# Loading ScalarE's function table ahead of two small input transfers in a single-core decode layer

## The chip, the cores and the metric

The kernel runs on one core of a Trainium2 chip. The metric is the time of one execution on the device in microseconds (us); smaller is better.

## The reference

One decoding step for four sequences: adaptive layer norm, attention over a window of cached keys and values, adaptive layer norm again, and a feed-forward block with ReLU. Everything is bfloat16. Cut to what matters:

```python
W = min(4096, max(256, Sk // 4))           # 1024 cached positions, 8 key/value heads, 32 query heads
mod = (silu(c) @ w_mod).reshape(4, 6, 1, -1)
sa, ca, ga, sb, cb, gb = (mod[:, i] for i in range(6))
h = layernorm(x) * (1 + ca) + sa
x = x + ga * attention(h, k_cache, v_cache, wq, wo)    # softmax over the last W positions
h = layernorm(x) * (1 + cb) + sb
x = x + gb * (relu(h @ w1) @ w2)
```

`c` and `x` (called `A_x`) are 4 x 512 numbers, 4 KB each. The weights and the two caches are 32 MB.

## The kernel before

SyncE issues all large loads in one queue, in the order of their use: two key blocks, the modulation weights `wmod_sb`, the query weights, six more key blocks, eight value blocks, the output weights, the feed-forward weights. ScalarE issues the two small transfers first and then loads its function table.

```python
cx_sb = work.tile([2 * B, D], bf16, name="cx_sb")
nc.scalar.dma_start(out=cx_sb[0:B, :], in_=c)
nc.scalar.dma_start(out=cx_sb[B:2 * B, :], in_=A_x.rearrange("b o d -> (b o) d"))
# ...
for gi in range(KAHEAD):                   # KAHEAD = 2
    load_k(gi)                             # 1 MiB each, on nc.sync
nc.sync.dma_start(out=wmod_sb[:], in_=w_mod.rearrange("(p t) n -> p t n", t=DT))   # 3 MiB
# ... wq, keys 2 to 7, values 0 to 7, wo, w1, w2: all on nc.sync
nc.scalar.preload_act_table_set("natural_log_exp_and_others")
# ... constants on GpSimd and VectorE
tp0 = psA.tile([P, DT, 2 * B], bf16, tag="t", name="tp0")
for t in range(DT):                        # L177: the first work of TensorE
    nc.tensor.transpose(out=tp0[:, t, :], in_=cx_sb[:, t::DT], identity=ident_bf[0:2 * B, 0:2 * B])
nc.scalar.activation(out=a_c[:], in_=cT, func=ACT.Abs)              # cT: the c half of tp0
nc.scalar.activation(out=t_c[:], in_=a_c[:], func=ACT.Exp, scale=-1.0)
# ... VectorE makes silu(c) of it: siluT32
kts_pending = [k_transposes(gi) for gi in range(KAHEAD)]            # L202: 64 transposes
# ... L236: the first matmuls that need siluT32 and wmod_sb
```

TensorE takes its instructions in program order: the transposes of `cx_sb`, the 64 transposes of the first two key blocks, then the modulation matmuls.

## Time and profile before

| Item | Before |
|---|---|
| Median time, in the rounds with the changed kernel | 85.91 us (85.81 to 85.98, 6 runs) |
| Span of the profiled run | 84.1 us |
| Moved by DMA | 32.13 MB |
| Last feed-forward weights landed | 79.42 us |
| `ACT_TABLE_LOAD` | 1.60 to 2.88 us |
| `cx_sb` first used by TensorE | 4.49 us |
| First key transposes | 5.99 us |
| Modulation matmuls (L236) start | 15.94 us, after 4.40 us of idle time |

The span runs from the first to the last instruction of the trace; the measured time is 1.8 us more. How to read the table: the first five microseconds belong to the change, the 4.40 us are the room behind it, and 79.42 us is the moment after which only a few microseconds of work remain. The prediction shows the lines themselves.

### The profile page before, as it was taken

What the parts mean: (1) busy time and instruction counts of PE and PEld (TensorE: products, weight loads), DVE (VectorE), ACT (ScalarE), POOL (GpSimd) and SP (SyncE); (2) the same over time, 40 slices, a digit from 0 to 9 for tenths busy, and PEclk for the clock granted to TensorE, in tenths of its full rate; (3) what the DMA queues carried; (4) which work ended last, traced back from release to release, by engine and by line L of the source; (5) the groups of instructions that cost most, each with busy time, mean ns of one, the idle gap of its engine ahead of it and who ended that gap; (6) DMA issues with size and microseconds to landing.
All of it is one profiled execution on the core that took longest, in us unless ns stands there. A gap on an engine that the chain in (4) does not pass through costs nothing.

```text
span 84.1 us, 2367 instructions
## 1 busy us (share of the span) xinstructions
PE 57.5 (68%) x1064; PEld 47.4 (56%) x1064; DVE 26.4 (31%) x73; ACT 23.5 (28%) x37; POOL 5.2 (6%) x20
## 2 busy tenths in 40 slices
PE   0029940499729899999999329996454478598840
PEld 0029940248629739977778029996452058588720
DVE  0144480030330103645665768500003020241420
ACT  2314670003020004977798196300000010001000
POOL 6980000000000000000000000000000000000000
PEclk9999999957955555999999995696555555555555
DMA  0999998999999999999999999999999999999500
GB/s 2 333 401 452 503 421 386 444 421 444 421 394 405 433 433 413 413 413 425 425 413 409 425 425 421 405 433 421 425 409 409 425 432 425 413 398 406 210 0 2
DMA packets 4077, 32.13 MB, mean 382 GB/s; under 512 B 476, under 2 KB 612, under 8 KB 996
## 3 DMA queue, kind: packets, MB, share of 16 engines
q1 hardware_dynamic: 4052, 31.99, 91.7%
q8 instruction: 8, 0.13, 0.6%
q10 hardware_dynamic: 16, 0.01, 0.0%
q14 instruction: 1, 0.01, 0.0%
HBM read 31.99 MB, written 0.00 MB: 381 GB/s over the span
## 4 chain that ended last, share of the span: by engine, by line
DMA 64%; PE 25%; DVE 3%; issue 2%; SPq 1%; ACT 1%; DVEq 0%
DMA w<-in_B_w_dram 24%; DMA v<-in_A_v_cache_dram 24%; DMA wmod_sb<-in_w_mod_dram 16%; PE ktp L202 9%; PE qT_ps L302 4%; PE sc_ps L214 4%; PE mT L253 2%; PE mT L255 2%; PE z_ps L470 2%; PE m_ps L236 2%; SPq L81 1%; PE m_ps L239 1%; PE gb_ps L244 1%; PE st_ps_var L269 1%; ACT lnv L286 0%
## 5 line engine op out<-in xcount | busy, mean ns | idle before, releaser
L202 PEld LDWEIGHTS <-k 128*128 128x128 bf16 x256 | 17.3, 110 | 3.9 <-issue 2.5
L202 PE MATMUL ktp<-ident_k,k 128*128 128x128 bf16 x256 | 18.4, 241 | 1.2 <-DMA k<-in_A_k_cache_dram 1.2
L207 ACT COPY kT<-ktp 128x1024 bf16<-128x1024 bf16 x16 | 15.5, 1016 | 13.2 <-PE ktp L202 12.1
L205 DVE COPY kT<-ktp 128x1024 bf16<-128x1024 bf16 x16 | 11.1, 691 | 11.6 <-PE ktp L202 11.3
L340 PE MATMUL oT_ps<-pT,v 128*128 128x16 bf16 x256 | 7.3, 172 | 2.5 <-issue 1.9
L340 PEld LDWEIGHTS <-v 128*128 128x128 bf16 x256 | 7.1, 100 | 2.7 <-issue 2.0
L214 PE MATMUL sc_ps<-kT,qpad 128*32 128x512 bf16 x64 | 5.6, 445 | 0.4 <-DVE qpad L306 0.4
L357 PE MATMUL pT_ps<-ident_bf,p_rep 128*128 128x128 bf16 x32 | 3.1, 278 | 2.9 <-DVE p_rep L351 2.9
L357 PEld LDWEIGHTS <-p_rep 128*128 128x128 bf16 x32 | 2.7, 127 | 3.4 <-DVE p_rep L351 3.4
L302 PE MATMUL qT_ps<-hT,wq_sb 128*128 128x4 bf16 x128 | 3.6, 166 | 1.4 <-DVE ab L295 1.4
L302 PEld LDWEIGHTS <-wq_sb 128*128 128x128 bf16 x128 | 3.5, 104 | 1.5 <-issue 1.5
L236 PE MATMUL m_ps<-wmod_sb,siluT 128*32 128x512 bf16 x16 | 1.3, 435 | 4.4 <-DMA wmod_sb<-in_w_mod_dram 4.4
L409 ACT COPY y<-y_ps 128x256 f32<-128x256 f32 x1 | 0.4, 372 | 11.4 <-DVE y L408 11.4
L404 PE MATMUL y_ps<-wo_sb,o 128*32 128x512 bf16 x16 | 2.1, 619 | 2.0 <-DMA wo_sb<-in_A_wo_dram 1.1
L177 PE MATMUL tp<-ident_bf,cx_sb 8*128 8x8 bf16 x4 | 0.3, 168 | 4.5 <-DMA cx_sb<-in_A_x_dram 4.5
L236 PEld LDWEIGHTS <-siluT 128*32 128x32 bf16 x16 | 0.4, 95 | 4.7 <-issue 4.5
L382 DVE TENSOR_TENSOR oT_sb<-oT_ps,rb 128x128 bf16<-128x128 f32 x1 | 0.3, 292 | 8.6 <-PE oT_ps L340 8.6
L416 PEld LDWEIGHTS <-wo_sb 128*128 128x128 bf16 x64 | 2.5, 121 | 0.6 <-DMA wo_sb<-in_A_wo_dram 0.6
L416 PE MATMUL y_ps<-o,wo_sb 128*128 128x4 bf16 x64 | 2.4, 173 | 0.5 <-DMA wo_sb<-in_A_wo_dram 0.5
L177 PEld LDWEIGHTS <-cx_sb 8*128 8x128 bf16 x4 | 0.2, 110 | 4.5 <-issue 4.5
L351 DVE TENSOR_TENSOR p_rep<-e_sb,mi 128x512 int32<-128x512 int32 x4 | 2.5, 685 | 0.7 <-ACT e_sb L346 0.7
L459 PE MATMUL u_ps<-ab,w 128*128 128x8 bf16 x56 | 2.4, 181 | 0.4 <-DMA w<-in_B_w_dram 0.4
(107 smaller groups left out, 57.0 us busy)
## 6 DMA issues: line engine op xcount, KB each, us to landing
k<-in_A_k_cache_dram SPq DMA_DIRECT2D x8, 1024.0 KB, 25.8
v<-in_A_v_cache_dram SPq DMA_DIRECT2D x8, 1024.0 KB, 19.9
wq_sb<-in_A_wq_dram SPq DMA_DIRECT2D x2, 2048.0 KB, 18.0
wo_sb<-in_A_wo_dram SPq DMA_DIRECT2D x4, 1024.0 KB, 19.9
wmod_sb<-in_w_mod_dram SPq DMA_DIRECT2D x1, 3072.0 KB, 13.7
w<-in_B_w_dram SPq DMA_DIRECT2D x1, 1792.0 KB, 21.7
w<-in_B_w_dram SPq DMA_DIRECT2D x1, 768.0 KB
w<-in_B_w_dram SPq DMA_DIRECT2D x1, 640.0 KB, 20.1
```

What stands on the lines that cost most here:

```text
L202: nc.tensor.transpose(out=tp[:, ii, :], in_=k_tiles[gi][:, iq * IQ + ii, :], identity=ident_k)
L205: nc.vector.tensor_copy(out=dst, in_=tp[:])
L207: nc.scalar.copy(out=dst, in_=tp[:])
L214: nc.tensor.matmul(out=sc_ps[hw * CG:(hw + 1) * CG, half * HALF:(half + 1) * HALF], lhsT=qpad[:, b, par, hw, :], rhs=kT[:, half * (NI // 2 ...
L236: nc.tensor.matmul(out=m4_ps[k * CG:(k + 1) * CG, :], lhsT=siluT32[:, t, :], rhs=wmod_sb[:, t, k * D:(k + 1) * D], start=(t == 0), stop=(t ...
L302: nc.tensor.matmul(out=qT_v[:, hq, :], lhsT=wq_sb[:, t, hq * Dh:(hq + 1) * Dh], rhs=hT[:, t, :], start=(t == 0 and hq == 0), stop=(t == DT ...
L340: nc.tensor.matmul(out=oT_ps[:, hw, par].rearrange("p b r -> p (b r)"), lhsT=v_tiles[h][:, i, :], rhs=pT[:, i, c0:c0 + B * rep], start=(fi ...
L351: nc.vector.tensor_tensor(out=p_w[:, ws, :], in0=e_w[:, ws].unsqueeze(2).to_broadcast([P, WQ // 2, B]), in1=mi4[:].unsqueeze(1).to_broadca ...
L357: nc.tensor.transpose(out=tp[:, ii, :], in_=p_rep[:, i // 2, :, i % 2], identity=ident_bf[:])
L404: nc.tensor.matmul(out=y4_ps[q0:q0 + CG, :], lhsT=o4[:, l, g % 2, g // 2, :], rhs=wo_sb[:, g, l, :], start=(g == 0 and l < 4), stop=(g == ...
L416: nc.tensor.matmul(out=y_ps[:, m, :], lhsT=wo_sb[:, g, l, m::DT], rhs=o4[:, l, g % 2, g // 2, 0:B], start=False, stop=(g == NP - 1 and l = ...
L459: nc.tensor.matmul(out=u_ps[:, m - m0].rearrange("p s b -> p (s b)"), lhsT=w1_cols(t, m), rhs=ab[:, t].rearrange("p s b -> p (s b)"), star ...
```

## The change

The intent is to have the table ready as early as possible: the load is the first instruction of ScalarE, and the two small transfers are issued behind it. The risk is that they have to wait for it.

```diff
+    nc.scalar.preload_act_table_set("natural_log_exp_and_others")
 
     cx_sb = work.tile([2 * B, D], bf16, name="cx_sb")
     nc.scalar.dma_start(out=cx_sb[0:B, :], in_=c)
@@
-    nc.scalar.preload_act_table_set("natural_log_exp_and_others")
     ident_bf = const.tile([P, P], bf16, name="ident_bf")
```

## The prediction

> **What bounds the kernel now.** I began with the page, to see whether any engine is near full, then read the chain of waits that ended last, and only then the first eight microseconds, where the change is.
>
> ```profile
> PE 57.5 (68%) x1064; PEld 47.4 (56%) x1064; DVE 26.4 (31%) x73; ACT 23.5 (28%) x37; POOL 5.2 (6%) x20
> DMA  0999998999999999999999999999999999999500
> DMA 64%; PE 25%; DVE 3%; issue 2%; SPq 1%; ACT 1%; DVEq 0%
> ```
>
> The first line is each engine's busy time and its share of the 84.1 us span. ScalarE (ACT) is busy for 28% and no compute engine is near full. The second is the DMA engines' busy share, in tenths, in 40 slices of 2.1 us: empty in the first slice, eight or nine tenths until the 37th, then over. The page gives 32.13 MB moved, 31.99 MB of it read from HBM. From about 2.0 us to the last landing at 79.42 us that is 32.1 / 77.4 = 415 GB/s, with no gap. The third is the chain's shares: 64% is transfers. So this kernel is one long input stream with a head (before the first byte) and a tail (after the last byte).
>
> The chain in order of time (start in us, length in us, what) shows both:
>
> ```profile
> 0.73 0.66 SPq L81
> ...
> 1.46 0.58 SPq L81
> ...
> 2.07 13.73 DMA wmod_sb<-in_w_mod_dram
> ...
> 39.39 19.88 DMA v<-in_A_v_cache_dram
> ...
> 59.28 20.14 DMA w<-in_B_w_dram
> ...
> 79.46 1.31 PE z_ps L470 x30
> ```
>
> The head is the SyncE queue (SPq) issuing the first two key transfers. ScalarE's two small transfers, `c` and `A_x`, are not on this chain at all, nor is the table load. The tail is 30 matmuls, 0.30 and 0.29 us of VectorE and the output transfer. The measured 85.94 us is 1.84 us more than the span, a part that the change does not enter.
>
> Now the start (timeline: start, length, engine, line, what; in brackets idle time before it and what ended it):
>
> ```profile
> 0.73 0.55 ACTq L71 DMA_DIRECT2D cx_sb<-in_c_dram  x1
> 0.73 1.30 SPq L81 DMA_DIRECT2D k<-in_A_k_cache_dram  x2
> 1.31 0.26 ACTq L72 DMA_DIRECT2D cx_sb<-in_A_x_dram  x1
> 1.60 1.28 ACT L129 ACT_TABLE_LOAD   x1 [1.60 <-PEq L498]
> 4.49 0.26 PE L177 MATMUL tp<-ident_bf,cx_sb 8*128 8x8 bf16 x4 [4.49 <-DMA cx_sb<-in_A_x_dram]
> 4.78 0.18 ACT L180 ACTIVATE a_c<-tp 128x16 f32<-128x16 bf16 x1 [1.90 <-PE tp L177]
> 5.99 5.37 PEld L202 LDWEIGHTS <-k 128*128 128x128 bf16 x64 [1.33 <-DMA k<-in_A_k_cache_dram]
> 6.58 0.23 DVE L189 TENSOR_TENSOR siluT<-tp,f_c 128x16 bf16<-128x16 bf16 x1
> 15.94 1.27 PE L236 MATMUL m_ps<-wmod_sb,siluT 128*32 128x512 bf16 x16 [4.40 <-DMA wmod_sb<-in_w_mod_dram]
> ```
>
> The load runs from 1.60 to 2.88 us, and ScalarE then idles 1.90 us until the transposes of `cx_sb` have finished on TensorE. So its early end is worth nothing today: it is already hidden behind the landing of `A_x`. The next two gaps are the cushions of this branch. TensorE waits until 5.99 us for the first key block whatever happens to `cx_sb`. It then sits idle 4.40 us before the modulation matmuls (L236), which wait for the 3 MB `wmod_sb`. `siluT`, the product of the small transfers, is ready at 6.58 + 0.23 = 6.81 us and first used at 15.94 us, 9.1 us later.
>
> **What the Trainium skill says.** "ScalarE: Activation LUTs", section "What ACT_TABLE_LOAD costs", gives about 1283 ns for the load and about 1380 ns for a drain, 2.66 us a switch. The trace agrees on the load (1.28 us); the drain is not visible, since ScalarE's next work waits for TensorE until 4.78 us. "Perfetto Trace Analysis", section "Sequencer Loop", says that the sequencer pushes engine instructions into a queue and starts control instructions itself. A transfer issued behind a table load then would not have to wait for the load to end. The trace before cannot confirm this: ScalarE issues nothing after its load. The same page, in its HWDGE section, says that the descriptor generator is shared by the two issuing queues and locked for one at a time. The trace agrees in kind: `c` took 0.55 us to issue beside the first key transfer, `A_x` 0.26 us. "DMA: Bandwidth & Descriptors", section "Queues, rings and completion order", says that each DMA engine alternates between the queues packet by packet, so two 4 KB transfers should not sit behind megabytes of another queue. Here they were used at 4.49 us, before the first key block landed, with the key queue already full; one instance, in agreement.
>
> **The change part by part.** Nothing is removed or added; three ScalarE instructions change order.
>
> *Table load to the front.* It starts where `c` started, 0.73 us, and ends near 0.73 + 1.28 = 2.01 instead of 2.88 us. Gain on the path: nothing, for `a_c` waits for TensorE.
>
> *Small transfers behind it.* From the end of the `A_x` issue (1.31 + 0.26 = 1.57 us) to its use (4.49 us) is 2.92 us; I keep that delay. Three cases:
> (a) the issue only waits for the load to be handed over: a few hundredths later, use near 4.5 us;
> (b) the issue waits for the load's end at 2.01: two issues at 0.26 to 0.4 us each, done near 2.6 to 2.8, use near 5.5 to 5.7, transposes done by about 6.0, just as the first key block lands;
> (c) it waits for the skill's drain too: all of (b) 1.38 us later, use near 7.1, and the key transposes start near 7.4 instead of 5.99, 1.4 us late.
> I take (a), at about even odds, because of the sequencer section; but the answer hardly depends on it. The worst, 1.4 us, comes out of 4.40 us of idle time before L236 and leaves 3.0. `siluT` would be ready near 9.5 against 15.94 us. In none of the cases does it get to the chain.
>
> *Issue on the SyncE side.* The first key issue took 0.66 us, with `c` being issued beside it. The third to eighth key transfers took mostly 0.53 or 0.54 us where they stood alone in the timeline. If the sharing cost the first 0.66 - 0.54 = 0.12 us, and `c` now comes behind, the whole stream may start about 0.1 us earlier. This is the only term on the path, and I count 0.08 of it.
>
> Sum: 85.94 - 0.08 = 85.86; I predict 85.85 us.
>
> **Rivals.** *A later wait in the transfer queue.* In the program of before the transfers take eight completion semaphores in turn, in the order `c`, k0, `A_x`, k1, `wmod_sb`, two of `wq_sb`, k2; then k3 must wait for `c`, k4 for k0, k5 for `A_x`, k6 for k1 and k7 for `wmod_sb`. The SyncE queue's own waits show the ones that bite:
>
> ```profile
> SPq L81 <- DMA wmod_sb<-in_w_mod_dram: 6.8, 1, 6.8
> SPq L81 <- DMA k<-in_A_k_cache_dram: 2.4, 2, 1.3
> ```
>
> (waiter, what it waits for, us in total, times, longest.) With `c` and `A_x` later, k3 and k5 may be issued later, and if the two small transfers move in the order, k5 may even wait for `wmod_sb`, until 15.8 us. That would hurt only if the queue ran dry. Before k3 there are k0, k1, `wmod_sb`, `wq_sb` and k2 in it: 1 + 1 + 3 + 4 + 1 = 10 MiB, 10.5 MB, or 25 us at 415 GB/s. Even with k5 held to 15.8 us, 4 MiB of `wq_sb` and 3 MiB of keys are still in front, 17 us. So 0 us; were I wrong, and the stream stopped for a microsecond, 86.9 us.
>
> *The branch of the small transfers becomes the bound.* That takes more than 4.4 us of push on TensorE's key transposes, that is, `cx_sb` usable later than about 10 us. Nothing in the trace makes it so late; it would cost what it overshoots, say 86.5 us.
>
> *ScalarE becomes a bound early,* because its evacuations of the key transposes (first at 7.07 us) slide. They share the same 4.40 us. About 85.9 us.
>
> *A shorter head.* If the head is cut by the whole extra 0.12 us and the 0.04 of the second issue (0.58 against 0.54), 85.78 us. No larger gain is in reach: the stream still has its 77 us.
>
> **Range and chances.** The three runs of before lie within 0.17 us. Adding a tenth or two for the head and for a stream that differs a little from build to build gives 85.55 to 86.15. Faster by over 2% needs 84.2 us, which means 1.7 us out of a head whose only movable term is 0.16: 1%. Slower by over 2% needs 87.7 us, more than the worst rival that I can build: 2%. The rest, 97%, is within 2%.
>
> **What would show it.** Right: the load at 0.73 us and 1.28 us long; the chain still from key issue to `wmod_sb`, values and the last weights, landing near 79.3 to 79.5 us; L236 still released by `wmod_sb` near 15.8 us; the first key issue near 0.55 us. The start of the `c` issue tells (a), (b) and (c) apart: near 0.8, near 2.0, near 3.4 us. Wrong: a zero in the DMA row between slices 2 and 37, L236 released by `siluT`, or the first key block landing well away from 5.97 us.

## The result and the profile after

The changed kernel took 86.00 us in the median (85.82 to 86.07, 6 runs), against 85.91 us before. The ratio is 1.0007, with a 95% interval of 0.9993 to 1.002: the same. Ratios here are the mean time of one kernel's runs over that of the other's of the same rounds, so not quite the ratio of the medians that are quoted.

These are the busy times, the DMA row and the shares of the chain from the page after:

```profile
PE 57.6 (68%) x1064; PEld 47.4 (56%) x1064; DVE 26.3 (31%) x73; ACT 23.5 (28%) x37; POOL 5.2 (6%) x20
DMA  0999998999989999999999999999999999999500
DMA 64%; PE 26%; DVE 3%; issue 2%; SPq 1%; ACT 1%; DVEq 0%
```

No busy time has moved by more than 0.1 us, no share by more than one per cent, and the DMA row has no new gap. The timeline of the start of the changed kernel shows what did move (start, length, engine, line, what):

```profile
0.73 1.28 ACT L69 ACT_TABLE_LOAD   x1 [0.73 <-PEq L498]
0.76 0.55 ACTq L72 DMA_DIRECT2D cx_sb<-in_c_dram  x1
1.34 0.26 ACTq L73 DMA_DIRECT2D cx_sb<-in_A_x_dram  x1
4.55 0.26 PE L177 MATMUL tp<-ident_bf,cx_sb 8*128 8x8 bf16 x4 [4.55 <-DMA cx_sb<-in_A_x_dram]
4.84 0.18 ACT L180 ACTIVATE a_c<-tp 128x16 f32<-128x16 bf16 x1 [2.83 <-PE tp L177]
15.84 1.49 PE L236 MATMUL m_ps<-wmod_sb,siluT 128*32 128x512 bf16 x16 [4.46 <-DMA wmod_sb<-in_w_mod_dram]
```

The load starts at 0.73 instead of 1.60 us. The issue of `c` starts at 0.76 us, 0.03 us after the load has started and 1.25 us before it ends: the queue of ScalarE (ACTq) did not wait for the load. So `cx_sb` is used at 4.55 instead of 4.49 us, and ScalarE, with its table ready 0.87 us earlier, idles 2.83 us before its first activation where it idled 1.90. The gain became idle time, because what ended the wait was TensorE's transposes, as before. L236 is still released by `wmod_sb`.

The end of the chain of waits in the changed kernel (start, length, what):

```profile
39.55 19.82 DMA v<-in_A_v_cache_dram
...
59.38 20.17 DMA w<-in_B_w_dram
...
79.60 1.31 PE z_ps L470 x32
```

The last weights land at 79.56 us (before: 79.42), and the span is 84.2 us (84.1). That 0.1 us is inside the scatter of the spans of the six runs, 84.0 to 84.2.

### The profile page after: what moved, and what is told of

Read it like the earlier page. It is cut to its first block, busy times and chain, and to the rows that moved or that the text cites. A ratio compares the mean times of both kernels' runs of the same rounds, so it can differ in the third digit from the quotient of the medians.

```text
span 84.2 us, 2367 instructions
## 1 busy us (share of the span) xinstructions
PE 57.6 (68%) x1064; PEld 47.4 (56%) x1064; DVE 26.3 (31%) x73; ACT 23.5 (28%) x37; POOL 5.2 (6%) x20
## 4 chain that ended last, share of the span: by engine, by line
DMA 64%; PE 26%; DVE 3%; issue 2%; SPq 1%; ACT 1%; DVEq 0%
DMA w<-in_B_w_dram 24%; DMA v<-in_A_v_cache_dram 24%; DMA wmod_sb<-in_w_mod_dram 16%; PE ktp L202 9%; PE qT_ps L302 4%; PE sc_ps L214 4%; PE m_ps L236 2%; PE mT L253 2%; PE z_ps L470 2%; PE mT L255 1%; SPq L82 1%; PE m_ps L239 1%; PE gb_ps L244 1%; PE st_ps_var L269 1%; ACT lnv L286 0%
## 5 line engine op out<-in xcount | busy, mean ns | idle before, releaser
L207 ACT COPY kT<-ktp 128x1024 bf16<-128x1024 bf16 x16 | 15.5, 1015 | 12.8 <-PE ktp L202 11.8
L357 PE MATMUL pT_ps<-ident_bf,p_rep 128*128 128x128 bf16 x32 | 3.3, 290 | 2.9 <-DVE p_rep L351 2.9
L357 PEld LDWEIGHTS <-p_rep 128*128 128x128 bf16 x32 | 2.9, 135 | 3.4 <-DVE p_rep L351 3.4
L302 PE MATMUL qT_ps<-hT,wq_sb 128*128 128x4 bf16 x128 | 3.7, 166 | 1.4 <-DVE ab L295 1.4
L236 PE MATMUL m_ps<-wmod_sb,siluT 128*32 128x512 bf16 x16 | 1.5, 503 | 4.5 <-DMA wmod_sb<-in_w_mod_dram 4.5
L302 PEld LDWEIGHTS <-wq_sb 128*128 128x128 bf16 x128 | 3.6, 104 | 1.5 <-issue 1.5
L236 PEld LDWEIGHTS <-siluT 128*32 128x32 bf16 x16 | 0.4, 101 | 4.8 <-issue 4.6
```

Of the source, the lines that this page charges most:

```text
L207: nc.scalar.copy(out=dst, in_=tp[:])
L236: nc.tensor.matmul(out=m4_ps[k * CG:(k + 1) * CG, :], lhsT=siluT32[:, t, :], rhs=wmod_sb[:, t, k * D:(k + 1) * D], start=(t == 0), stop=(t ...
L302: nc.tensor.matmul(out=qT_v[:, hq, :], lhsT=wq_sb[:, t, hq * Dh:(hq + 1) * Dh], rhs=hT[:, t, :], start=(t == 0 and hq == 0), stop=(t == DT ...
L357: nc.tensor.transpose(out=tp[:, ii, :], in_=p_rep[:, i // 2, :, i % 2], identity=ident_bf[:])
```

## The experiments

"The same" fits two stories. One: the change has no effect on the small transfers, so nothing follows. Two: the small transfers could come several microseconds later and still nothing would follow. The experiments ask how much the branch may slip, what a slip really costs, and what a table load costs when it is not hidden. The line numbers of held0 to held20 are five higher than those of the changed kernel (L241 there is L236), those of held4_rows seven higher; those of no_preload are one lower than in the kernel before.

**held0: the small transfers wait for the end of the load.** From the changed kernel:

```diff
     cx_sb = work.tile([2 * B, D], bf16, name="cx_sb")
+    hold = const.tile([P, 1024], f32, name="hold")
+    nc.vector.memset(hold[:], 0.0)
+    nc.scalar.copy(out=cx_sb[0:1, 0:16], in_=hold[0:1, 0:16])
     nc.scalar.dma_start(out=cx_sb[0:B, :], in_=c)
```

Expected:

> The two small transfers are held until ScalarE's table load has really ended: one small ScalarE copy behind the load writes a corner of cx_sb, and the c transfer must wait for it (numbers in cx_sb are overwritten by c, so the result stays right). c should be issued near 2.3 us instead of 0.76, and cx_sb used near 5.9 instead of 4.55 us. Main theory (the branch has more than 4 us of cushion): key transposes start near 6.2 instead of 5.98, L236 still waits for wmod_sb near 15.8, time 85.9 to 86.0. Rival (table and transfers are on the path): up to 1.4 us longer, 87.3. Second question, the issue times: if the c issue slows the first key issue by sharing the descriptor generator, the first key issue is now 0.54 us and c about 0.26; if a queue's first issue is simply longer, they stay at 0.66 and 0.55.

Measured: 85.91 us (85.85 to 85.92, 4 runs) against 85.88 us, ratio 1.0001 (0.9986 to 1.0016). From the timeline of held0:

```profile
2.25 0.54 ACTq L77 DMA_DIRECT2D cx_sb<-in_c_dram  x1
7.74 0.26 PE L182 MATMUL tp<-ident_bf,cx_sb 8*128 8x8 bf16 x4 [7.74 <-DMA cx_sb<-in_A_x_dram]
```

This is the slow case (b) of the prediction, and the time is the same. L241 starts at 15.85 us, released by `wmod_sb`, with 2.35 us of idle time left in front of it. But `cx_sb` was used at 7.74 us, not near 5.9, and the key transposes began at 7.93, not near 6.2: from the end of the `A_x` issue (3.09 us) it took 4.65 us, not 2.92. The second question is answered against sharing: the first key issue, now without any issue of ScalarE beside it, still took 0.65 us, and `c` took 0.54 us.

**held4: held back further.** As held0, with four ScalarE copies of 128 x 1024 numbers in front of the small copy:

```diff
     nc.vector.memset(hold[:], 0.0)
+    for _ in range(4):
+        nc.scalar.copy(out=hold[:], in_=hold[:])
     nc.scalar.copy(out=cx_sb[0:1, 0:16], in_=hold[0:1, 0:16])
```

Expected:

> As held0 with four ScalarE copies of 1024 elements (about 1.04 us each) in front of the small one: c issued near 6.5 us, cx_sb used near 9.5, key transposes start near 9.8 instead of 5.98 us, 3.8 us late. The idle time before L236 was 4.46 us, so the cushion theory says that about 0.6 us of it are left, L236 still released by wmod_sb, time 85.9 to 86.1. The rival, no cushion, says about 89.8.

Measured: 86.24 us (86.21 to 86.33, 4 runs) against 85.88 us, ratio 1.0043 (1.0028 to 1.0058). From the timeline of held4:

```profile
7.16 0.26 ACTq L78 DMA_DIRECT2D cx_sb<-in_A_x_dram  x1
14.73 0.26 PE L182 MATMUL tp<-ident_bf,cx_sb 8*128 8x8 bf16 x4 [14.73 <-DMA cx_sb<-in_A_x_dram]
20.51 1.05 PE L241 MATMUL m_ps<-wmod_sb,siluT 128*32 128x512 bf16 x16
```

The issue came where it was expected, but `cx_sb` was usable only 7.31 us after its end. So this run went further than planned: the key transposes were 8.94 us late (14.92 against 5.98), and L241 started at 20.51 instead of 15.84 us, 4.67 us late, no longer waiting for any transfer (there is no bracket behind it). The expectation that it would still wait for `wmod_sb` was missed. Even so the spans are 84.1 to 84.2 us, those of the kernel before, and the last weights land at 79.41 us. A delay of 4.67 us behind the room of 4.46 us was taken up in full before the end. The 0.36 us by which the time grew lie outside the span: it is 2.1 us more than the span in each of the four runs, where it is 1.8 us in the kernel before. What these 0.3 us are stays open.

**held10 and held20: held back until it must hurt.** The same edit with `range(10)` and `range(20)`. Expected of held10:

> Ten copies: c issued near 12.7 us, cx_sb used near 15.7, key transposes 9.9 us late, so L236 about 5.4 us late. Theory A, the rival as the prediction put it (the overshoot over the 4.4 us is paid in full): about 91.4 us. Theory B (later waits of TensorE for transfers, 0.8 + 1.2 + 0.5 + 0.4 + 0.3 us before values, output and FFN weights, and perhaps 1.8 more, take up part, because the stream of transfers goes on): 86.5 to 88.3 us, with the last weights landing still near 79.5 us.

Expected of held20:

> Twenty copies: c issued near 23 us, cx_sb used near 26, key transposes 20 us late, L236 about 15.8 us late. Theory A: about 101.8 us. Theory B: the same minus 3 to 5 us, 97 to 99 us; TensorE should wait for no transfer after L236. The transfer queue holds k0, k1, wmod_sb, wq_sb, k2 and k3 before the first transfer that waits for a small one, 11.5 MB or 28 us, so the DMA row should show no gap before about 45 us even now; later gaps may come from buffers that the keys free late.

Measured: held10 90.23 us (89.59 to 90.74, 4 runs), ratio 1.0501 (1.0449 to 1.0553); held20 99.59 us (98.87 to 100.22, 4 runs), ratio 1.162 (1.158 to 1.166). Both branches were later than expected (9.83 and 18.54 us instead of 5.4 and 15.8), because the small transfers again landed late. So the times expected beforehand do not decide: held10 lies outside theory B's 86.5 to 88.3 us and nearer to theory A's 91.4. The modulation matmuls of held10 and the DMA row of the page of held20:

```profile
25.67 1.05 PE L241 MATMUL m_ps<-wmod_sb,siluT 128*32 128x512 bf16 x16
```

```profile
DMA  4799989999999999999999999999999991000000
```

| | L236/L241 late against the changed kernel | paid (median against before) | taken up |
|---|---|---|---|
| held0 | 0.0 us | 0.0 us | all |
| held4 | 4.67 us | 0.36 us, none of it in the span | 4.3 us or more |
| held10 | 9.83 us | 4.35 us | 5.5 us |
| held20 | 18.54 us | 13.71 us | 4.8 us |

Set against the lateness that was really reached, theory A, that all lateness behind the first room is paid, is refuted: it would give 90.6 us for held4, 95.7 for held10 and 104.4 for held20. Theory B holds in kind: about five microseconds more are taken up downstream. The table sets the lateness of the profiled run against the median of four; in the profiled runs alone the span grew by 4.4 us (held10, 88.6) and 12.8 us (held20, 97.0), so that 5.4 and 5.7 us were taken up.

Where they come from can be read in two stretches. From the first transposes of the softmax result (L357, or L362) to the end of the span it takes 34.4 us in the changed kernel, 30.4 in held10 and 30.6 in held20, 3.8 to 4.0 us less. In the changed kernel TensorE's matmuls wait in this stretch for values, output weights and feed-forward weights for 0.76 + 1.16 + 0.48 + 0.40 + 0.30 = 3.1 us; in held10 and held20 not once. The other 0.7 to 0.9 us are not accounted for. The rest is a faster middle: from the start of L236 to those transposes it takes 33.96 us in the changed kernel, 32.50 in held10 and 32.03 in held20, so 1.5 to 1.9 us less. Most of that lies right behind L236: up to the first query matmul (L302) it takes 9.47 us in the changed kernel, at a granted clock (the share of its full speed that TensorE was given) of 0.70 in this stretch, 8.04 in held10 at 0.87 and 8.15 in held20 at 0.80. The same stretch took 7.91 us in held0 at 0.89, and 11.53 in load_behind_abs (below) at 0.50. So the time goes with the granted clock; that the clock is the cause is argued, since no run sets it alone.

The DMA row of held20 is cut in slices of 97.0 / 40 = 2.4 us. It is full until slice 33, which is about 80 us, and the stream ends near 81 us, one to two microseconds later than before. Even with `cx_sb` held to 29 us it had no gap that shows, only a lower rate between 50.9 and 60.6 us (375 GB/s against 420 in the changed kernel, about one microsecond of stream): the SyncE queue waited for `c` (1.9 us in all) and for the transposes that free key buffers (21.2 us), but there were always megabytes issued in front of it. The end, 16 us later, is set by the engines alone.

**load_behind_abs: a table load in the open.** From the kernel before:

```diff
-    nc.scalar.preload_act_table_set("natural_log_exp_and_others")
@@
     nc.scalar.activation(out=a_c[:], in_=cT, func=ACT.Abs)
+    nc.scalar.preload_act_table_set("natural_log_exp_and_others")
```

Expected:

> From the kernel before: the table load now comes behind the first activation (Abs), with its own wait for nothing else, so that it lies in the open between Abs and Exp; the build puts one more load, of another set, in front of Abs, where it is hidden. This measures the exposed cost: Exp starts after Abs (about 5.0 us) plus 1.3 us if a switch costs the load alone, plus 2.7 us if a drain of 1.38 us belongs to it. siluT ready near 8.1 or 9.5 instead of 6.81 us, used at 15.9. Main theory (cushion): time 85.9 to 86.1, no matter which. Rival (a late table load reaches the end): 87.2 to 88.6.

Measured: 85.92 us (85.77 to 85.95, 4 runs) against 85.93 us, ratio 0.9994 (0.9977 to 1.0012). From ScalarE's timeline:

```profile
4.76 0.18 ACT L179 ACTIVATE a_c<-tp 128x16 f32<-128x16 bf16 x1 [1.89 <-PE tp L176]
4.97 1.28 ACT L180 ACT_TABLE_LOAD   x1
6.26 0.21 ACT L182 ACTIVATE t_c<-a_c 128x16 f32<-128x16 f32 x1
```

A switch between two activations costs 1.28 us and some hundredths: `Exp` starts 0.01 us after the load's end. The drain of 1.38 us of the prediction's case (c) does not show. `siluT` was ready at 7.42 + 0.23 = 7.65 us, and the time is the same: a load in the middle of this branch is as free as one at its head. The slower stretch behind L236 that was named above, 2.1 us longer than in the changed kernel, was free as well.

**no_preload: loads where the program cannot hide them.** From the kernel before:

```diff
-    nc.scalar.preload_act_table_set("natural_log_exp_and_others")
```

The build then adds five loads by itself. Expected:

> From the kernel before: no explicit load; the build then puts five, of two sets, in front of Abs, of each of the two Ln and of the Exp behind each Ln. The first is hidden as before. The two at the first layernorm lie in the chain from L236 to the scores (near 24 us), the two at the second behind s_ps (near 75 us), before ffn1. If the theory holds that only what lies behind the last weights' landing, or pushes TensorE past all later waits for transfers, is paid, then the first pair (about 1.3 or 2.6 us exposed) is taken up by later waits and costs 0 to 1 us, and the second pair delays ffn1 (u_ps, near 76 us) by about 2.6 us; ffn1 ends near 79.1 us today and z_ps waits 0.3 us for the last weights, so that some 2 us are paid: 87.5 to 89. If loads are hidden wherever they stand: 86.0.

Measured: 86.97 us (86.21 to 87.14, 4 runs) against 85.93 us, ratio 1.0098 (1.0043 to 1.0152). From ScalarE's timeline of the second layer norm:

```profile
71.14 1.28 ACT L445 ACT_TABLE_LOAD   x1
77.31 0.30 ACT L445 ACTIVATE mm<-mm,eps_t 128x4 f32<-128x4 f32 x1 [4.89 <-DVE mm L444]
77.63 1.28 ACT L446 ACT_TABLE_LOAD   x1
78.92 0.20 ACT L446 ACTIVATE rstd<-mm 128x4 f32<-128x4 f32 x1
```

The load before `Ln` ran at 71.14 us, six microseconds before its activation had its data. The load before `Exp` had the `Ln` in front of it and was paid. I had counted both as exposed, so the expectation of 87.5 to 89 us was too high. At the first layer norm both loads were exposed (26.15 and 27.76 us): there the built program has a wait for VectorE's result in front of the load, and at the second layer norm the wait is on `Ln` itself, behind the load. `z_ps` started at 79.86 us and ran without a wait for weights, to 81.6 us instead of 80.8 in the kernel before. The exposed loads are not its only lateness in this profiled run: from the first modulation matmul to those of the variance it took 9.53 us at a granted clock of 0.50, where the kernel before took 7.44 at 0.77. The same 2.1 us cost nothing in load_behind_abs; here the loads and the slow stretch together may have used up the slack, and the runs do not separate them. Three runs at a granted clock of 0.703 to 0.707 took 86.96 to 87.14 us, with spans of 84.9 to 85.1; the one at 0.733 took 86.21, with the span of the kernel before, 84.1. Such a dependence on the clock would fit a kernel whose end is set by TensorE; four runs are few. And 0.1 to 0.3 us of the loss lie outside the span, which is 2.0 to 2.1 us shorter than the time.

**held4_rows: what delays a small transfer.** From held4:

```diff
-    nc.sync.dma_start(out=wmod_sb[:], in_=w_mod.rearrange("(p t) n -> p t n", t=DT))
+    wmod_src = w_mod.rearrange("(p t) n -> p t n", t=DT)
+    for t in range(DT):
+        nc.sync.dma_start(out=wmod_sb[:, t, :], in_=wmod_src[:, t, :])
```

Expected:

> held4 with one more edit: wmod_sb comes in four transfers with rows of 6 KB instead of one with rows of 24 KB. In the runs with held transfers, from the end of the A_x issue to the use of cx_sb took 4.65 us beside key rows of 8 KB (held0), 7.31 us beside the 24 KB rows of wmod_sb (held4), 5.42 us at the change from wmod_sb to the 16 KB rows of wq_sb (held10) and 4.37 us near the end of wq_sb (held20). Theory R (a small transfer waits for rows of the other queue that are under way, so the wait grows with their size): 4 to 5 us here, cx_sb used near 11.5 to 12.5 us. Rival (it waits for bytes already queued, whatever the rows): again about 7.3 us, near 14.7. Time in either case that of held4 or less: 85.9 to 86.3.

Measured: 86.68 us (86.63 to 86.81, 4 runs) against 85.96 us, ratio 1.0084 (1.0069 to 1.0099). From the timeline of held4_rows:

```profile
11.83 0.26 PE L184 MATMUL tp<-ident_bf,cx_sb 8*128 8x8 bf16 x4 [11.83 <-DMA cx_sb<-in_A_x_dram]
```

The issue of `A_x` ended at 7.41 us, so it took 4.42 us, where the same issue at the same time took 7.31 us beside rows of 24 KB. Theory R's prediction of 4 to 5 us holds; the rival's 7.3 us does not. The edit also changes the number of transfers and with it the semaphores, so these two runs alone leave the size of the rows the likely, not the only possible, cause.

The packets settle more of it. The kept traces hold every DMA packet with its start, length and size. The two small transfers are 8 packets of 1 KB and 8 of 4 bytes, and they run among packets of the SyncE queue, each of which is one row:

| | SyncE's packets meanwhile | one takes (median) | first packet of `c` to the end of the last of `A_x` |
|---|---|---|---|
| held4_rows | 6 KB | 0.23 us | 0.94 us |
| held0 | 8 KB | 0.31 us | 1.09 us |
| held20 | 8 KB | 0.31 us | 1.24 us |
| held10 | 16 KB | 0.61 us | 2.04 us |
| held4 | 24 KB | 0.91 us | 3.74 us |

The four groups of small packets (the data of `c`, the 4 bytes behind them, the same for `A_x`) begin about one large packet apart: at 10.40, 11.36, 12.27 and 13.22 us in held4, and at 10.30, 10.58, 10.81 and 11.08 us in held4_rows. So in this part theory R is shown, in four runs with the same number of transfers and one with more. It also explains the 4.37 us of held20: its packets stood beside key rows of 8 KB, not beside `wq_sb` as the expectation took it. The other part does not go with the rows: the first packet of `c` starts 2.8 to 3.3 us after the end of its issue in all five runs, and 0.4 us after it in the changed kernel, where the stream has not yet begun. Its cause stays open. (The packets' clock may lie half a microsecond off that of the instructions; the comparison of runs does not depend on it.)

The kernel itself is slower than held4, not faster as I expected: its span is 84.5 us, the last weights land at 79.72 us, 0.3 us later than in held4, and it too has some 2.2 us outside the span. Why is open.

**swap_cx: which issue is the long one.** From the changed kernel, the two lines of the small transfers exchanged:

```diff
-    nc.scalar.dma_start(out=cx_sb[0:B, :], in_=c)
     nc.scalar.dma_start(out=cx_sb[B:2 * B, :], in_=A_x.rearrange("b o d -> (b o) d"))
+    nc.scalar.dma_start(out=cx_sb[0:B, :], in_=c)
```

Expected:

> The changed kernel with the two small transfers in the other order, A_x first. If the first issue of a queue is the longer one whatever it carries, A_x now takes about 0.55 us and c 0.26; if the c transfer itself is the costly one, c keeps 0.55. The first key issue stays at 0.66 us. cx_sb used near 4.5 us, time 85.8 to 86.1.

Measured: 85.97 us (85.92 to 86.16, 4 runs) against 85.96 us, ratio 0.9997 (0.9981 to 1.0014). From ScalarE's timeline:

```profile
0.76 0.55 ACTq L72 DMA_DIRECT2D cx_sb<-in_A_x_dram  x1
1.34 0.26 ACTq L73 DMA_DIRECT2D cx_sb<-in_c_dram  x1
```

`A_x` is now the long one. The first issue of ScalarE's queue takes 0.55 us whatever it carries. The first key issue stayed at 0.66 us, as expected; `cx_sb` was used at 4.73 us, 0.2 us later than expected, without effect.

No version came out of this that beats the two kernels.

## Why the prediction was right, point by point

**The bound.** Right. The stream of loads ends at 79.4 to 79.6 us in both kernels, and near 81 us even in held20. That only a shorter stream, head or tail would have shortened the time follows from the chain of waits; no run here shortens one of them.

**The load at the front.** Right: 0.73 us, 1.28 us long, and the earlier end turned into idle time (2.83 us, of which 1.90 were there).

**Case (a) for the small transfers.** Right: the issue of `c` came at 0.76 us, beside the load. The prediction took this case at even odds, so this was half luck; the time did not depend on it, as held0 shows for the other case. The start times fit a sequencer that passes the load on and goes to the next instruction, but show nothing of its inside.

**The cushion.** Right, and too small: the prediction allowed a lateness of 4.4 us at the key transposes. held4 was 8.94 us late there without a longer span.

**The delay of 2.92 us that (b) and (c) kept.** This step failed: "I keep that delay." held0 is case (b), and it measured 4.65 us; further on it was 7.31 us. The argument that two small transfers do not sit behind megabytes came from one instance at the very start, when the stream had only just begun. The small packets did get their turns among the large ones, but each turn cost one row of the other queue, up to 0.91 us, and the first turn came about 3 us after the issue. Had (b) come true, `cx_sb` would have been used at 7.7 rather than 5.5 to 5.7 us. It would still have cost nothing, as held0 shows, so the forecast did not depend on it.

**The 0.12 us of sharing, of which 0.08 were counted.** This step failed: "If the sharing cost the first 0.66 - 0.54 = 0.12 us". The first key issue takes 0.64 to 0.66 us in every kernel, whether ScalarE's first issue starts beside it or only at 2, 7, 13 or 24 us; the sign that the prediction named, "the first key issue near 0.55 us", did not come. Nor was the 0.55 us of `c` a sign of a shared generator, as the prediction read it: in held4 `c` took 0.55 us with no SyncE issue beside it. The swap shows that on ScalarE's queue the first issue is the long one (0.55 against 0.26 us); that the first key issue is long for the same reason is the likely reading. Without this term the sum is 85.94 us. The measured ratio, 1.0007, says that the true term is near zero.

**The rival of a later wait in the transfer queue.** Rightly put at 0 us. In the changed program the order of the semaphores is k0, `c`, `A_x`, k1, so that k4 and k5 wait for the small transfers. In held4 the SyncE queue did wait 3.8 us for `c` and 1.4 us for `A_x`, and the last weights came no later.

**The rival of the branch as the bound.** Its price was mis-sized: "it would cost what it overshoots". About the first five microseconds of overshoot cost nothing in the span, mostly because TensorE later stands waiting for transfers; beyond that nearly each microsecond is paid (from held10 to held20 8.71 us more lateness, 8.4 us more span).

## What to carry to other kernels

A setup instruction is worth moving only if something waits for it: look at what ended the idle time behind it, here a matmul that waited for data, and the gain can be read off as zero. In a kernel that streams its weights, the slack of an early branch is not only the idle time in front of its first consumer: the later waits for transfers add to it (here 3.1 us of the 5.4 to 5.7 taken up), so look at those too before you price a delay. Issue small inputs first: at the start they were usable 2.9 us after their issue, in the running stream 4.4 to 7.3 us.

## What the Trainium skill lacked or had wrong

- "ScalarE: Activation LUTs", "What ACT_TABLE_LOAD costs": a load of about 1283 ns is right (1.28 us in every run). The further drain of about 1380 ns was not there: in load_behind_abs `Abs` ended at 4.94 us, the load ran from 4.97 to 6.25, and `Exp` began at 6.26; in no_preload `Ln` ended at 27.74, the load ran from 27.76 to 29.04, and `Exp` began at 29.05.
- The same page does not say whether a load holds up transfers issued behind it by ScalarE. Here it did not: the issue started 0.03 us after the load's start. "Perfetto Trace Analysis", "Sequencer Loop", leads to the right answer.
- "DMA: Bandwidth & Descriptors", "Queues, rings and completion order", describes the alternation of queues but gives no delay for a small transfer in a busy stream. Here it was 4.65 us beside rows of 8 KB, 7.31 us beside rows of 24 KB and 4.42 us once these came as 6 KB, against 2.92 us at the start; one turn cost 0.23 us (6 KB) to 0.91 us (24 KB).
- No page that I read gives a longer first issue of a queue: 0.55 against 0.26 us for 4 KB on ScalarE, 0.64 to 0.66 against mostly 0.54 to 0.58 us for 1 MiB of keys on SyncE (the fourth in the kernel before took 0.64 too).
